# Decode attention with queries and probabilities as narrow stationary operands in four TensorE column groups

## The chip, the core and the metric

The program runs on one core of one Trainium2 chip. The metric is device time in microseconds (us) of one launch. The kernel before was timed three times: 375.3, 375.79 and 376.94 us, median 375.79 us. The profile is of a further execution, which took 379.11 us.

## What is computed

Two transformer layers are applied twice to four single tokens, with the same weights and the same caches in both passes. Cut to what matters:

```
x = A_x                                   # B=4 tokens, D=512
for pass in (1, 2):
    xn = layernorm(x)
    q  = (xn @ wq)  -> 32 heads of 128    # four query heads share one key/value head
    s  = q . k_cache * 128**-0.5          # per token 8 kv heads x 4096 keys x 128
    p  = softmax(s)
    x  = x + (p @ v_cache) @ wo
    xn = layernorm(x)
    x  = x + (gelu(xn @ w_gate) * (xn @ w_up)) @ w_down     # F=1792
return x
```

Everything is bf16 in memory. The key cache and the value cache are 33.5 MB each (4 tokens x 8 heads x 4096 x 128). The weights are 13.6 MB together.

## The kernel before

**Tiles.** A key or value tile is half of one kv head: 2048 rows, 512 KB, laid as 128 partitions x 16 rows x 128. `load_kv` (L101) issues each as one DMA on SP's queue into the pool `kvin`, which has `KV_BUFS = 7` buffers shared by keys and values. One queue carries everything, so the order of the calls in the program is the order of the transfers.

**Keys** (`keys`, L209). A head's 32 blocks of 128x128 are transposed on TensorE (L218: the key block is stationary, the identity streams), eight at a time into a PSUM tile `tp` (three buffers). `evac` copies each to SBUF as `kt`, two in five on ScalarE (L205), the rest on VectorE (L207). The pool `ktp` holds eight heads. They stay there, because pass 2 of the same token uses them again: keys are read from memory once.

**Scores** (`scores`, L222). The transposed key block is the stationary operand and the four query columns of its group stream past it: 32 matmuls of 4 columns for each head, result with the keys on the partitions. Two heads make a group (`GH = 2`, four groups `NGRP`), which has one `softmax` (L231): maximum along the free axis, `partition_all_reduce` on GpSimd, subtraction, exponential on ScalarE, sum, a second `partition_all_reduce`, reciprocal.

**Values** (`values`, L254). A block of 128 value rows is stationary, four probability columns stream past it: 32 matmuls of 4 columns for each head, accumulated in `ot` (one PSUM buffer), then one VectorE multiplication by the reciprocal writes the head's output, already transposed, into `OT_bf` (L264). Values are read twice, once in each pass.

**Order of the work.** The loop over tokens (L280) does pass 1 group by group: keys of two heads, scores, softmax, and the values of the group before. Then come the output projection (L159), the FFN (L164), a layer norm and the projection of pass 2's queries (`q_proj`, L303, 128 matmuls). Pass 2 of a token is deferred: its scores and softmaxes are done at once (L307), but its values are read after the next token's `q_proj` (L304 to L306), or for the last token at the end (L308). The `kt` buffers of a token come free only when its pass-2 scores are done. The framework's scheduler fixes the order on each engine when the program is built: it may take up work that comes later in the program where, by its own estimate, that work is ready, so matmuls of different steps are interleaved on TensorE. On the chip each engine then runs its instructions in that fixed order.

Of the kernel before, what the change touches and what calls it, by code (L numbers as in the profile page):

```python
# [8 lines left out]
FP32 = mybir.dt.float32  # L9
BF16 = mybir.dt.bfloat16  # L10
I32 = mybir.dt.int32
ACT = mybir.ActivationFunctionType
ALU = mybir.AluOpType
AX = mybir.AxisListType
RED = bass_isa.ReduceOp
# [6 lines left out]
GH = 2  # L22
KV_BUFS = 7
# [3 lines left out]
def kernel(  # L27
# [28 lines left out]
    NGRP = Hkv // GH  # L56
    assert Hkv % GH == 0 and C % CH == 0 and CH % TB == 0
    assert GH * C * rep * 4 <= 2048 and KF * B * 4 <= 2048 and Hq * B * 4 <= 2048
# [7 lines left out]
    p1p = ctx.enter_context(tc.tile_pool(name="p1p", bufs=3))  # L66
    p2p = ctx.enter_context(tc.tile_pool(name="p2p", bufs=NGRP + 1))
    shp = ctx.enter_context(tc.tile_pool(name="shp", bufs=2))
    grp = ctx.enter_context(tc.tile_pool(name="grp", bufs=2 * NGRP))
# [4 lines left out]
    ps_misc = ctx.enter_context(tc.tile_pool(name="ps_misc", bufs=2, space=bass.MemoryType.PSUM))  # L74

    ident_bf = const.tile([P, P], BF16, name="ident_bf")
    make_identity(nc, ident_bf[:])
    mean_f = const.tile([P, P], FP32, name="mean_f")
# [16 lines left out]
    q2_bf = state.tile([P, B, Hq], BF16, name="q2_bf")  # L95
# [44 lines left out]
    def q_proj(b0, nb, q_bf, parts):  # L140
        bs = slice(b0, b0 + nb)
        hp = Hq // parts
        for part in range(parts):
            qps = ps_misc.tile([P, hp, nb], FP32, name="qps", tag="misc")
            for i in range(hp):
                m = part * hp + i
                for k in range(KD):
                    nc.tensor.matmul(qps[:, i, :], lhsT=wq_sb[:, k, m * Dh:(m + 1) * Dh],  # L148
                                     rhs=xn_bf[:, bs, k], start=(k == 0), stop=(k == KD - 1))
            nc.vector.tensor_copy(  # L150
                out=q_bf[:, bs, part * hp:(part + 1) * hp].rearrange("p b h -> p h b"),
                in_=qps[:])
# [45 lines left out]

    KT = {}
# [9 lines left out]
    def keys(b, kvh):  # L209

        kt = ktp.tile([P, C, P], BF16, name="kt", tag="kt")
        KT[kvh] = kt
        for t in range(NT):
            kn = load_kv(A_k_cache, b, kvh, t, "k_t")
            for g in range(CH // TB):
                tp = ps_tp.tile([P, TB, P], BF16, name="tp", tag="tp")
                for i in range(TB):
                    nc.tensor.transpose(tp[:, i, :], kn[:, g * TB + i, :], ident_bf[:, :])  # L218
                c0 = t * CH + g * TB
                evac(kt[:, c0:c0 + TB, :], tp[:])  # L220

    def scores(b, g, q_bf):  # L222
        sc = ps_sc.tile([P, GH, C, rep], FP32, name="sc", tag="sc")
        for s in range(GH):
            kvh = g * GH + s
            for c in range(C):
                nc.tensor.matmul(sc[:, s, c, :], lhsT=KT[kvh][:, c, :],  # L227
                                 rhs=q_bf[:, b, kvh * rep:(kvh + 1) * rep], start=True, stop=True)
        return sc

    def softmax(sc, pool):  # L231
        colmax = grp.tile([P, GH, rep], FP32, name="colmax", tag="colmax", bufs=2)
        nc.vector.tensor_reduce(out=colmax[:], in_=sc.rearrange("p s c h -> p s h c"),  # L233
                                axis=AX.X, op=ALU.max)
        gmax = grp.tile([P, GH, rep], FP32, name="gmax", tag="gmax", bufs=2)
        nc.gpsimd.partition_all_reduce(gmax.rearrange("p s h -> p (s h)"),  # L236
                                       colmax.rearrange("p s h -> p (s h)"), P, RED.max)
        sh = shp.tile([P, GH, C, rep], FP32, name="sh", tag="sh")
        nc.vector.tensor_tensor(out=sh[:], in0=sc[:],  # L239
                                in1=gmax[:].unsqueeze(2).broadcast_to([P, GH, C, rep]),  # L240
                                op=ALU.subtract)
        pe = pool.tile([P, GH, C, rep], BF16, name="pe", tag="pe")
        nc.scalar.activation(out=pe[:], in_=sh[:], func=ACT.Exp, scale=scale)  # L243
        ssum = grp.tile([P, GH, rep], FP32, name="ssum", tag="ssum", bufs=2)
        nc.vector.tensor_reduce(out=ssum[:], in_=pe.rearrange("p s c h -> p s h c"),  # L245
                                axis=AX.X, op=ALU.add)
        den = grp.tile([P, GH, rep], FP32, name="den", tag="den", bufs=2)
        nc.gpsimd.partition_all_reduce(den.rearrange("p s h -> p (s h)"),  # L248
                                       ssum.rearrange("p s h -> p (s h)"), P, RED.add)
        rden = grp.tile([P, GH, rep], FP32, name="rden", tag="rden")  # L250
        nc.vector.reciprocal(out=rden[:], in_=den[:])
        return pe, rden

    def values(b, kvh, prob, o_bf):  # L254
        pe, rden = prob
        s = kvh % GH
        ot = ps_ot.tile([P, rep], FP32, name="ot", tag="ot")
        for t in range(NT):
            v = load_kv(A_v_cache, b, kvh, t, "v_t")
            for i in range(CH):  # L260
                c = t * CH + i
                nc.tensor.matmul(ot[:], lhsT=v[:, i, :], rhs=pe[:, s, c, :],  # L262
                                 start=(c == 0), stop=(c == C - 1))
        nc.vector.tensor_tensor(out=o_bf[:, b, kvh * rep:(kvh + 1) * rep], in0=ot[:],  # L264
                                in1=rden[:, s], op=ALU.mult)
# [4 lines left out]
    hq0 = GH * rep * Dh  # L270
# [8 lines left out]
    prob2_prev = None  # L279
    for b in range(B):  # L280
        prob1 = {}
        for g in range(NGRP):
            for s in range(GH):
                keys(b, g * GH + s)
            if b == 0 and g == 0:
                dq.dma_start(out=wq_sb[:, :, hq0:], in_=wq_dram[:, :, hq0:])
                q_proj(0, B, q1_bf, NGRP)
            prob1[g] = softmax(scores(b, g, q1_bf), p1p)
            if b == 0 and g == NGRP - 1:
                dq.dma_start(out=wo_sb[:], in_=A_wo.rearrange("(i p) n -> p i n", p=P))  # L290
            if g > 0:
                for s in range(GH):
                    values(b, (g - 1) * GH + s, prob1[g - 1], OT_bf)
        for s in range(GH):
            values(b, (NGRP - 1) * GH + s, prob1[NGRP - 1], OT_bf)
# [7 lines left out]
        q_proj(b, 1, q2_bf, 2)  # L303
        if prob2_prev is not None:  # L304
            for kvh in range(Hkv):
                values(b - 1, kvh, prob2_prev[kvh // GH], OT2_bf)  # L306
        prob2_prev = [softmax(scores(b, g, q2_bf), p2p) for g in range(NGRP)]  # L307
    for kvh in range(Hkv):  # L308
        values(B - 1, kvh, prob2_prev[kvh // GH], OT2_bf)
# [41 lines left out]
```

## Time and profile before

| | |
|---|---|
| median of three runs | 375.79 us |
| the profiled execution, whole | 379.11 us |
| its span, first to last instruction | 377.3 us |
| TensorE (PE) busy | 275.4 us, 73% |
| VectorE (DVE), ScalarE (ACT), GpSimd (POOL) busy | 137.5, 67.7, 25.0 us |
| mean granted TensorE clock | 0.648 |
| moved by DMA | 115.59 MB, 306 GB/s over the span |
| key transposes (L218), matmuls and busy time | 1024, 97.2 us |
| score matmuls (L227) | 2048, 69.3 us |
| value matmuls (L262) | 2048, 69.0 us |

PE is TensorE's matmul side and PEld its weight loads, which overlap. SPq is the queue on SP that issues the DMAs; a wait of SPq is a transfer that could not be issued yet. PEclk is the share of full speed that TensorE was granted. A group's busy time is the time in which at least one of its instructions ran, and the mean beside it is the length of one, from issue to end, so for pipelined matmuls the count times the mean is much more than the busy time.

### The profile page before, as it was taken

How to read it: one execution, taken by the hardware profiler on the slowest of the kernel's cores; microseconds unless marked ns; L12 is line 12 of the kernel's file. 1: busy time of each engine (PE TensorE's matmuls, PEld its weight loads, DVE VectorE, ACT ScalarE, POOL GpSimd, SP SyncE). 2: the span in 40 equal slices, each digit the busy share in tenths (PEclk: the TensorE clock that was granted, in tenths of full speed). 3: DMA queues.
4: the chain of work that ended last, by engine and by line, in shares of the span. 5: the costliest groups of instructions: out<-in, count | busy, mean ns of one | idle time of the engine just before them, and what ended most of it. 6: DMA issues, size and time to landing. Idle time of an engine off the chain costs nothing.

```text
span 377.3 us, 15723 instructions
## 1 busy us (share of the span) xinstructions
PE 275.4 (73%) x7268; PEld 263.8 (70%) x7268; DVE 137.5 (36%) x476; ACT 67.7 (18%) x90; POOL 25.0 (7%) x70
## 2 busy tenths in 40 slices
PE   0978872645999897578888885697978866785645
PEld 0878862535998896577788785697978865775545
DVE  0534440032456442333463433334534332351032
ACT  1314230000143330001242230001423400010000
POOL 0000000000112000001100000011010000020000
PEclk9999685555558667555596685555778855555555
DMA  7998999999258999947899999758999998579920
GB/s 283 413 370 271 387 353 382 406 377 394 83 164 269 384 347 347 386 122 220 279 407 406 356 361 410 244 179 241 404 365 349 377 373 302 156 218 347 407 109 4
DMA packets 35762, 115.59 MB, mean 306 GB/s; under 512 B 3176, under 2 KB 9072, under 8 KB 35696
## 3 DMA queue, kind: packets, MB, share of 16 engines
q1 hardware_dynamic: 35696, 114.58, 83.0%
q8 instruction: 57, 0.93, 1.0%
q14 instruction: 9, 0.07, 0.0%
HBM read 114.56 MB, written 0.00 MB: 304 GB/s over the span
## 4 chain that ended last, share of the span: by engine, by line
PE 53%; DMA 16%; DVE 15%; issue 9%; ACT 3%; POOL 3%; SPq 1%; POOLq 0%; ACTq 0%; DVEq 0%
PE tp L218 19%; PE sc L227 14%; DMA v_t<-in_A_v_cache_dram 9%; PE ot L262 7%; DMA wd_sb<-in_B_w_down_dram 6%; PE qps L148 4%; DVE kt L207 2%; PE yT L159 2%; PE hg L170 2%; DVE colmax L233 2%; DMA k_t<-in_A_k_cache_dram 2%; DVE ssum L245 2%; ACT kt L205 2%; ACT pe L243 1%; PE st L114 1%
## 5 line engine op out<-in xcount | busy, mean ns | idle before, releaser
L218 PE MATMUL tp<-ident_bf,k_t 128*128 128x128 bf16 x1024 | 97.2, 271 | 1.2 <-DMA k_t<-in_A_k_cache_dram 0.6
L218 PEld LDWEIGHTS <-k_t 128*128 128x128 bf16 x1024 | 85.2, 125 | 2.0 <-issue 1.0
L262 PE MATMUL ot<-pe,v_t 128*128 128x4 bf16 x2048 | 69.0, 166 | 17.0 <-DMA v_t<-in_A_v_cache_dram 9.7
L262 PEld LDWEIGHTS <-v_t 128*128 128x128 bf16 x2048 | 63.0, 102 | 19.1 <-DMA v_t<-in_A_v_cache_dram 11.0
L227 PE MATMUL sc<-q_bf,kt 128*128 128x4 bf16 x2048 | 69.3, 166 | 9.1 <-DVE kt L207 3.1
L227 PEld LDWEIGHTS <-kt 128*128 128x128 bf16 x2048 | 64.4, 102 | 12.8 <-DVE kt L207 5.3
L205 ACT COPY kt<-tp 128x1024 bf16<-128x1024 bf16 x52 | 52.6, 1012 | 111.0 <-PE tp L218 93.9
L207 DVE COPY kt<-tp 128x1024 bf16<-128x1024 bf16 x76 | 51.7, 687 | 53.2 <-PE tp L218 51.6
L159 PEld LDWEIGHTS <-wo_sb 128*128 128x128 bf16 x640 | 22.4, 102 | 27.8 <-issue 18.6
L159 PE MATMUL yT<-OT_bf,wo_sb 128*128 128x1 bf16 (+1 forms) x640 | 22.2, 165 | 25.5 <-DVE OT_bf L264 16.4
L243 ACT ACTIVATE pe<-sh 128x256 bf16<-128x256 f32 x32 | 13.3, 417 | 99.0 <-DVE sh L239 72.9
L236 POOL PARTITION_ALL_REDUCE gmax<-colmax x32 | 11.8, 369 | 266.6 <-DVE colmax L233 262.0
L264 DVE TENSOR_TENSOR OT_bf<-ot,rden 128x4 bf16<-128x4 f32 x64 | 9.6, 149 | 53.4 <-PE ot L262 53.4
L148 PE MATMUL qps<-xn_bf,wq_sb 128*128 128x1 bf16 (+1 forms) x640 | 18.4, 165 | 8.2 <-DVE xn_bf L136 6.6
L148 PEld LDWEIGHTS <-wq_sb 128*128 128x128 bf16 x640 | 17.9, 104 | 8.8 <-DVE xn_bf L136 7.1
L233 DVE TENSOR_REDUCE colmax<-sc 128x8 f32<-128x256 f32 x32 | 13.6, 424 | 28.0 <-PE sc L227 25.9
L239 DVE TENSOR_TENSOR sh<-sc,gmax 128x256 f32<-128x256 f32 x32 | 13.5, 423 | 11.0 <-POOL gmax L236 10.8
L170 PE MATMUL hg<-xn_bf,wg_sb 128*128 128x1 bf16 (+1 forms) x280 | 8.2, 165 | 10.8 <-DVE xn_bf L136 5.8
L245 DVE TENSOR_REDUCE ssum<-pe 128x8 f32<-128x256 bf16 x32 | 13.3, 415 | 7.5 <-ACT pe L243 7.5
L248 POOL PARTITION_ALL_REDUCE den<-ssum x32 | 13.2, 413 | 39.7 <-DVE ssum L245 39.4
L170 PEld LDWEIGHTS <-wg_sb 128*128 128x128 bf16 x280 | 7.9, 104 | 11.2 <-DVE xn_bf L136 5.0
L194 PEld LDWEIGHTS <-wd_sb 128*128 128x128 bf16 x280 | 8.1, 104 | 8.8 <-issue 5.2
(95 smaller groups left out, 83.1 us busy)
## 6 DMA issues: line engine op xcount, KB each, us to landing
v_t<-in_A_v_cache_dram SPq DMA_DIRECT2D x128, 512.0 KB, 7.1
k_t<-in_A_k_cache_dram SPq DMA_DIRECT2D x64, 512.0 KB, 6.5
wo_sb<-in_A_wo_dram SPq DMA_DIRECT2D x1, 4096.0 KB, 18.8
wq_sb<-in_A_wq_dram SPq DMA_DIRECT2D x1, 3072.0 KB, 15.5
wg_sb<-in_B_w_gate_dram SPq DMA_DIRECT2D x1, 1792.0 KB, 12.3
wu_sb<-in_B_w_up_dram SPq DMA_DIRECT2D x1, 1792.0 KB, 16.3
wd_sb<-in_B_w_down_dram SPq DMA_DIRECT2D x1, 1792.0 KB, 20.9
wq_sb<-in_A_wq_dram SPq DMA_DIRECT2D x1, 1024.0 KB, 5.1
```

Source lines behind the costliest of these rows:

```text
L148: nc.tensor.matmul(qps[:, i, :], lhsT=wq_sb[:, k, m * Dh:(m + 1) * Dh], rhs=xn_bf[:, bs, k], start=(k == 0), stop=(k == KD - 1))
L159: nc.tensor.matmul(yT[:, :, dk], lhsT=wo_sb[:, i, dk * P:(dk + 1) * P], rhs=o_bf[:, bs, i], start=(i == 0 and dk == 0), stop=(i == Hq - 1 ...
L170: nc.tensor.matmul(hg[:, m, :], lhsT=wg_sb[:, k, m * P:(m + 1) * P], rhs=xn_bf[:, bs, k], start=(k == 0), stop=(k == KD - 1))
L205: nc.scalar.copy(out=out_ap, in_=in_ap)
L207: nc.vector.tensor_copy(out=out_ap, in_=in_ap)
L218: nc.tensor.transpose(tp[:, i, :], kn[:, g * TB + i, :], ident_bf[:, :])
L227: nc.tensor.matmul(sc[:, s, c, :], lhsT=KT[kvh][:, c, :], rhs=q_bf[:, b, kvh * rep:(kvh + 1) * rep], start=True, stop=True)
L233: nc.vector.tensor_reduce(out=colmax[:], in_=sc.rearrange("p s c h -> p s h c"), axis=AX.X, op=ALU.max)
L239: nc.vector.tensor_tensor(out=sh[:], in0=sc[:], in1=gmax[:].unsqueeze(2).broadcast_to([P, GH, C, rep]), op=ALU.subtract)
L243: nc.scalar.activation(out=pe[:], in_=sh[:], func=ACT.Exp, scale=scale)
L245: nc.vector.tensor_reduce(out=ssum[:], in_=pe.rearrange("p s c h -> p s h c"), axis=AX.X, op=ALU.add)
L262: nc.tensor.matmul(ot[:], lhsT=v[:, i, :], rhs=pe[:, s, c, :], start=(c == 0), stop=(c == C - 1))
```

## The change

**Scores.** A PSUM tile `sc` of 128 x 512 now holds the scores of four heads (`GH = 4`, two groups instead of four). Row 32j + 8s + 4b + h is head s of the group, query h, and key block 2j + b of 512 keys. The stationary operand is a 128x32 slice of a zero-padded query tile `zq` (28 zeros, four query columns, 28 zeros), placed so that the four queries fall on the wanted rows and the other 28 rows get zeros added. Eight matmuls for each head stream 512 key columns each; four successive ones write the four row blocks 32j, that is four column groups of the array. **Softmax** works on packed rows: one maximum for each row, masks (`onehot`, `maskneg`) to combine rows of one query through `partition_all_reduce`, one exponential that also sums, then four TensorE transposes and a copy give `pT`, keys on the partitions. **Values.** The stationary operand is a 128x32 slice of `pT`; 256 value columns (two row blocks of 128) stream past it, 16 matmuls for each head, again four column groups in turn. The result holds wanted and unwanted rows; ScalarE copies it to SBUF as f32, two f32 transposes on TensorE turn it, and VectorE sums the eight wanted blocks and multiplies by the reciprocal.

**Order.** Values of the deferred pass 2: one head after the next token's keys 1 and one after keys 2, the other six after its `q_proj`. **Buffers.** `kvin` goes from 7 to 6. The PSUM pool `ps_misc` (layer norm, projections, FFN) goes from two buffers to one, and a new one-buffer pool `ps_t` takes both kinds of new transposes. The first part of `wq`, loaded ahead of the first keys, is half of it (2 MB) instead of a quarter.

```diff
-GH = 2
-KV_BUFS = 7
+GH = 4
+ZP = 28
+KV_BUFS = 6
...
+    pTp = ctx.enter_context(tc.tile_pool(name="pTp", bufs=4))
+    osp = ctx.enter_context(tc.tile_pool(name="osp", bufs=1))
...
-    ps_misc = ctx.enter_context(tc.tile_pool(name="ps_misc", bufs=2, space=bass.MemoryType.PSUM))
+    ps_t = ctx.enter_context(tc.tile_pool(name="ps_t", bufs=1, space=bass.MemoryType.PSUM))
+    ps_misc = ctx.enter_context(tc.tile_pool(name="ps_misc", bufs=1, space=bass.MemoryType.PSUM))
...
+    def scores(sc, kvh, zq):
+
+        s = kvh % GH
+        for kbp in range(2):
+            off = ZP - rep * (2 * s + kbp)
+            for j in range(4):
+                nc.tensor.matmul(sc[32 * j:32 * j + 32, :], lhsT=zq[:, kvh, off:off + 32],
+                                 rhs=KT[kvh][:, 2 * j + kbp].rearrange("p c k -> p (c k)"),
+                                 start=(s == 0 and kbp == 0), stop=(s == GH - 1 and kbp == 1),
+                                 skip_group_check=True)
+
+    def softmax(sc):
+        m = grp.tile([P, 1], FP32, name="m", tag="m")
+        nc.vector.tensor_reduce(out=m[:], in_=sc[:], axis=AX.X, op=ALU.max)
...
+        nc.gpsimd.partition_all_reduce(gm[:], am[:], P, RED.max)
...
+        nc.scalar.activation(out=pr.rearrange("p c k -> p (c k)"), in_=sc[:], func=ACT.Exp,
+                             bias=nb[:, 0:1], scale=scale, accum_out=ls[:])
+        ptp = ps_t.tile([P, NCC, P], BF16, name="ptp", tag="t")
+        for cc in range(NCC):
+            nc.tensor.transpose(ptp[:, cc, :], pr[:, cc, :], ident_bf[:, :])
+        pT = pTp.tile([P, NCC, P], BF16, name="pT", tag="pT")
+        nc.vector.tensor_copy(out=pT[:], in_=ptp[:])
...
+        ot = ps_ot.tile([P, 2, Dh], FP32, name="ot", tag="ot")
         for t in range(NT):
...
+            for cl in range(CT):
+                cc = t * CT + cl
+                for j in range(4):
+                    nc.tensor.matmul(ot[32 * j:32 * j + 32, :, :],
+                                     lhsT=pT[:, cc, 32 * j:32 * j + 32], rhs=v[:, j, cl],
+                                     start=(cc == 0), stop=(cc == NCC - 1))
+        os = osp.tile([P, 2, Dh], FP32, name="os", tag="os")
+        nc.scalar.copy(out=os[:], in_=ot[:])
+        oT = ps_t.tile([P, 2 * P + 8], FP32, name="oT", tag="t")
+        for k in range(2):
+            nc.tensor.transpose(oT[:, k * P:(k + 1) * P], os[:, k, :], ident_f[:, :])
...
+        nc.vector.tensor_reduce(out=od[:], in_=sel, axis=AX.XY, op=ALU.add)
+        nc.vector.tensor_tensor(out=o_bf[:, b, kvh * rep:(kvh + 1) * rep], in0=od[:],
                                 in1=rden[:, s], op=ALU.mult)
...
+        for kvh in range(GH):
+            keys(b, kvh)
...
+            scores(sc, kvh, z1)
+            if kvh in (1, 2):
+                old_values(1)
+        p0 = softmax(sc)
+        sc = new_scores()
+        for kvh in range(GH, Hkv):
+            keys(b, kvh)
+            scores(sc, kvh, z1)
+            values(b, kvh - GH, p0, OT_bf)
+        p1 = softmax(sc)
...
+        for kvh in range(GH, Hkv):
+            values(b, kvh, p1, OT_bf)
...
+        old_values(Hkv)
+        prob2 = []
+        for g in range(2):
+            sc = new_scores()
+            for s in range(GH):
+                scores(sc, g * GH + s, zq2)
+            prob2.append(softmax(sc))
```

## The prediction, made before the changed kernel was run

> **What bounds the kernel now.** I read the page's engine lines first, then its slices, a table of busy time by stage, SPq's waits, and single stretches of TensorE's timeline.
>
> ```profile
> PE 275.4 (73%) x7268; PEld 263.8 (70%) x7268; DVE 137.5 (36%) x476; ACT 67.7 (18%) x90; POOL 25.0 (7%) x70
> ...
> PEclk9999685555558667555596685555778855555555
> DMA  7998999999258999947899999758999998579920
> ```
>
> TensorE is the busiest engine, but the DMA line stands at 9 except in four dips and at the end. The stage table cuts the span at the ends of output projections and at the next token's first key transposes (columns: PE, PEld, DVE, ACT, POOL busy; PEclk; DMA share; GB/s):
>
> ```profile
> 10.00:88.30 78.30, 51.34 (x1144) 48.98 (x1143) 27.05 (x87) 15.04 (x18) 3.09 (x8) 0.74 1.01 371
> ...
> 100.90:149.60 48.70, 43.77 (x1023) 42.51 (x1019) 23.00 (x57) 15.08 (x20) 5.71 (x15) 0.68 0.81 281
> 149.60:183.80 34.20, 23.74 (x812) 23.09 (x812) 12.60 (x62) 1.88 (x5) 3.01 (x8) 0.50 0.71 246
> 183.80:229.50 45.70, 38.97 (x903) 36.94 (x900) 19.59 (x47) 14.82 (x17) 3.05 (x8) 0.76 1.00 380
> ```
>
> Token 0 (first line) is all DMA: its weights come down the same queue. Pass 1 of tokens 1 and 2 (second and last line; token 3 took 44.9 us) is near both limits, with PE busy 85 to 90%. The stage after each (third line; 34.8 and 34.1 us for tokens 2 and 3) leaves the DMA at 0.71. SPq says why:
>
> ```profile
> SPq L104 <- PE ot L262: 100.6, 74, 5.7
> SPq L104 <- PE tp L218: 97.8, 59, 11.1
> ```
>
> A tile is fetched when TensorE is done with an older one. In the timeline, seven of the 16 value tiles of the deferred token are used before the queries are ready at 168.5, and nine after, among the scores; the next keys are transposed only at 183.8. The order of TensorE's queue bounds this stage.
>
> **Prices.** First two pieces of the chain, then two of the timeline, then the only f32 matmuls:
>
> ```profile
> 102.28 1.69 PE sc L227 x64
> 183.97 1.73 PE tp L218 x16
> ...
> 188.02 1.07 PE L218 MATMUL tp<-ident_bf,k_t 128*128 128x128 bf16 x16
> 188.93 0.34 PE L227 MATMUL sc<-q_bf,kt 128*128 128x4 bf16 x8
> ...
> L114 PE MATMUL st<-xx,mean_f x20: 350/362/422, 10.7 to 364.9; 128*128 128x8 f32 x16, 128*128 128x32 f32 x4
> ```
>
> A 4-column matmul takes 26 ns of queue time. A 128-column one takes 108 ns where the clock is 0.50 (0.84 ns a column), and 57 ns in the warm stretch, (188.93 - 188.02) / 16, 0.44 ns a column. In token 2's pass 1, L218 was busy 22.15 us for 256, 0.68 ns a column. The clock is 0.50 in stages of narrow matmuls only and 0.76 where 128-column ones are frequent; the change makes almost all attention work wide, so I take 0.56 ns, midway between 0.68 and 0.44.
>
> **What is removed** per head: 32 score and 32 value matmuls, 0.84 us each set. **What is added:**
>
> *Scores*: 8 matmuls x 512 columns. The trace has no two matmuls in different column groups. If four run together: 2 x 512 x 0.56 = 0.57 us; one after another: 2.29 us. The nearest row, narrow matmuls of 166 ns spaced 26 ns, shows that one need not end before the next starts, so I take together. *Values*: 16 x 256 columns, again 0.57 or 2.29 us.
>
> The Trainium skill, "TensorE: Matmul & The Clock Gate", Part 3, measured 2.38 times for three column tiles, 79% of perfect. By that figure (an estimate) the scores and the values of a head would cost 0.15 us more each, 128 x 0.15 = 19 us in all before what the DMA covers. Against the change, "TensorEngine Tiling (Array Packing)", Key Properties, says that switching between tiling modes drains the array, without a price; the kernel switches twice for every block of scores or values.
>
> *Fill at each such block*: an isolated matmul takes 166 ns instead of 26, so up to 0.14 us at each end, 0 to 0.28 us; I take 0.15, the middle. *f32 transposes*, two for each head's values: the layer norm's f32 matmul comes as two instructions (20 for 10 calls). From 8 to 32 columns it grows from 362 to about 410 ns, 2 ns a column, so 128 columns stream in 0.26 us; one transpose costs 0.26 us if it is one instruction, 0.52 if two. Two of them: 0.5 to 1.05, I take 0.9, nearer to the only f32 row. *Softmax*: four 128-column transposes, 0.3 us, 16 softmaxes instead of 32.
>
> So a head's values cost 0.57 + 0.15 + 0.9 = 1.6 us instead of 0.84, a head's scores 0.72 instead of 0.84.
>
> *Waits that are new on TensorE.* Between a head's values and its transposes stands ScalarE's copy of 128x256 (0.42 as L243, plus 0.2 us of handover on each side), 0.8 us; `ot` has one buffer, so the next head's values are held as well. While keys are in the queue they fill it; at the last four heads of a pass half is filled: 1.5 us. Between scores and values stand two VectorE steps, GpSimd's reduction, the exponential and the transposes: the like chain from 54.54 to 56.47 takes 1.9 us up to the end of the exponential, with 256 columns; with 512 and one more step about 3. The first softmax is covered by keys, the second not: 3 us.
>
> *Pass 1*, tokens 1 to 3, now with ten heads' values: keys 256 x 128 x 0.56 = 18.4, scores 8 x 0.72 = 5.8, values 10 x 1.6 = 16.2, softmax transposes 0.6, output projection 4.5 (as before), waits 4.5: 50.0 us. The DMA needs 36 tiles x 1.28 us (512 KB at the 410 GB/s of the fullest slices) = 46.1, so PE ends last. Against 48.7, 45.7 and 44.9: +1.3, +4.3, +5.1 = **+10.7**. Token 0: eight heads x 0.8 more lie in the 27 us in which PE idles there; **+2** for the first half, which has keys alone to transpose.
>
> *The stage after*: the FFN chain is the same. The deferred values shrink from 16 tiles to 12, so the first key tile is asked for four tiles earlier. After the queries: scores 8 x (2 x 512 x 0.84 ns + 0.15) = 8.1 us at clock 0.50, plus three heads at 2 us = 14 instead of 15.3, and the keys may start among them: -4 a token. `ps_misc` with one buffer makes the up projection wait for the gate's copy (0.17 plus handover) and the second half of the queries for the first's: +1. Three stages: **-9**.
>
> *End*: eight heads' values at 2.2 to 3 us against 2.56 us of DMA for two tiles: **+2**. Behind the last tile: copy, transposes, reduction and the single `ps_misc`: **+2.5**.
>
> *At nothing*: one buffer less (a lone tile lands in 3.5 us, so three in flight keep the queue full; if it bites, up to 1.3 us a stage); masks and zeros at the start, and 1 MB more of `wq` first, beside the first 9.9 us in which PE waits for the identity; VectorE and ScalarE (ScalarE gains 64 x 0.42 = 27 us on 67.7).
>
> Sum: 379.1 + 2 + 10.7 - 9 + 2 + 2.5 = 387.3 for the profiled execution, which stands 0.9% above the median; on the median's scale **384 us**.
>
> **Rivals.**
>
> *A, the forecast*: groups run together, pass 1 becomes TensorE's. 384, own range 372 to 400. 44%.
>
> *B, faster*: the wide streams keep the clock near full (0.44 ns) and the short scores let the next keys in early. Pass 1: 14.4 + 4.8 + 14 + 0.5 + 4.5 + 4 = 42, under the DMA's 46.1, so about 47: -1.7, +1.3, +2. The stage after: scores in 8 x 0.6 = 4.8 us, keys at 5 instead of 15 us behind the queries: -10 each. With +2 at the end 379.1 - 26 = 353, about 350 on the median's scale. For it: the clock line's 9 and 8 stand in key stages. Against: 0.50 whenever the FFN has just idled PE. It decides from about 0.50 ns a column, where pass 1 falls under the DMA. 30%.
>
> *C, slower by more*: no warm stretch (0.84), fills of 0.28, transposes of 1.05. Pass 1: 27.5 + 8 x 1.14 + 10 x 2.2 + 0.9 + 4.5 + 4.5 = 68, +66 in all; +9, +6 elsewhere: 460 at worst, with half of it 415. 16%.
>
> *D, the change doesn't do what it says*: the groups take turns. Each head's scores and values cost 1.72 us more, 32 times for each token, 220 us less what the DMA covers: 550 to 600. For it: no row shows otherwise. 10%.
>
> **Numbers.** A measurement of this kernel can tell about 0.5% from no change, 2 us. Faster: B and 0.09 of A, 0.39. Within: 0.09 of A. Slower: the rest, 0.52. The range leaves out D and the ends of B and C: 345 to 430.
>
> **What would show it.** Together or in turn: four score matmuls start within 0.1 us of each other, or 0.3 to 0.4 apart. f32 transposes: 128 instructions or 256, and PE busy of 0.5 or 1 us a head. Pass-1 stages: 50 us with the DMA share under 0.95 (A), 47 near 1.0 (B), 60 or more (C). Clock in pass 1: about 0.85 (A), near 1 (B). Stage after: 31 us (A) or 24 (B). I am wrong if pass 1 doesn't lengthen, or if the stage after grows because PE waits for ScalarE's copy with nothing to fill it.

## The result and the profile after

The changed kernel takes 393.73 us (median of four runs, 392.77 to 396.5) beside 376.37 us (375.3 to 380.78) for the kernel before in the same comparison. The ratio is 1.045, with a 95% interval of 1.035 to 1.0551: slower by 4.5%, where 2.2% was forecast. Times here are medians of all executions, while ratios and intervals use only those in the faster of two states that executions of one kernel fall into, so the two can differ by a few tenths of a percent. The profiled execution of it took 393.11 us, with a span of 391.4 us.

The engine lines and slices of the changed kernel's page:

```profile
PE 289.8 (74%) x4900; PEld 195.3 (50%) x4900; DVE 136.9 (35%) x538; ACT 90.6 (23%) x154; POOL 13.9 (4%) x38
...
PEclk9999995555699995558898985559999955575555
DMA  7978999999179999766699899567899997678800
```

TensorE issues a third fewer matmuls and is busy 14 us longer. Its clock is at 9 or 8 in the key stages. The DMA line has more 7s and 6s: bytes come more slowly although there are no more of them. The stage table (columns as before) for pass 1 of token 1, pass 1 of token 2, the stage after token 2, and pass 1 of token 3:

```profile
93.92:157.92 64.00, 52.06 (x845) 34.98 (x845) 25.81 (x83) 19.78 (x31) 3.31 (x8) 0.82 0.83 310
...
186.37:241.89 55.52, 43.37 (x651) 31.12 (x648) 20.95 (x58) 19.11 (x29) 2.09 (x5) 0.84 0.92 336
241.89:270.88 28.99, 24.89 (x476) 15.69 (x470) 10.30 (x60) 3.22 (x9) 1.21 (x3) 0.60 0.70 235
270.88:324.31 53.43, 41.22 (x651) 28.23 (x648) 21.11 (x58) 18.93 (x29) 2.09 (x5) 0.90 0.94 352
```

In pass 1 of token 2 PE is busy 43.4 of 55.5 us, and the DMA is no longer at 1.00: neither ends the stage alone. SPq waits longer for value matmuls, 142.8 us instead of 100.6:

```profile
SPq L126 <- PE ot L310: 142.8, 94, 4.3
```

Cut the same way in both profiled executions (each stage from the end of an output projection, or the first key transposes behind it, to the next such mark), the spans compare like this; the last column is the forecast's change. The row of token 1 also holds token 0's second queries and scores, in both kernels, because token 1's first keys are transposed ahead of them; the forecast's +1.3 was worked out from a cut that begins at 100.90:

| stage | before, us | after, us | change | forecast |
|---|---|---|---|---|
| token 0: pass 1, then its FFN | 65.7 + 15.3 | 70.8 + 13.1 | +2.9 | +2 |
| pass 1 of token 1 | 58.8 | 64.0 | +5.2 | +1.3 |
| pass 1 of token 2 | 45.4 | 55.5 | +10.1 | +4.3 |
| pass 1 of token 3 | 47.4 | 53.4 | +6.0 | +5.1 |
| stages after tokens 1 and 2 | 34.0 + 32.2 | 28.5 + 29.0 | -8.7 | -6 |
| last: the stage after token 3 and its deferred values | 55.5 | 53.7 | -1.8 | -1 |
| tail | 13.0 | 13.4 | +0.4 | +2.5 |
| span | 377.3 | 391.4 | +14.1 | +8.2 |

All of the miss lies in pass 1 of tokens 1 to 3: +21.3 instead of +10.7. The other stages did better than forecast by 4.7 us. (What of the +21.3 is only moved work is answered by e8 below.) The rest of the gap between 4.5% and 2.2% is that the two profiled executions stand differently to their medians: the one before 0.7% above, the one after 0.2% below.

What the 55.5 us of token 2's pass 1 hold, by TensorE's groups in that window (busy, mean ns, then the idle time before them and what ended it):

```profile
L250 PE MATMUL tp<-ident_bf,k_t 128*128 128x128 bf16 x256 | 19.8, 238 | 0.4 <-ACT kt L237 0.4
L310 PE MATMUL ot<-v_t,pT 128*32 128x256 bf16 x168 | 11.6, 318 | 1.4 <-DVE pT L288 1.4
L264 PE MATMUL sc<-kt,zq_0_129 128*32 128x512 bf16 x64 | 7.5, 383 | 3.5 <-ACT kt L237 2.0 <-DVE kt L239 1.1
L317 PE MATMUL oT<-ident_f,os 128*128 128x128 f32 x20 | 5.4, 360 | 5.2 <-ACT os L314 5.2
L188 PE MATMUL yT<-OT_bf,wo_sb 128*128 128x1 bf16 x128 | 4.6, 165 | 0.2 <-DVE OT_bf L323 0.2
L286 PE MATMUL ptp<-ident_bf,pr 128*128 128x128 bf16 x15 | 1.8, 245 | 1.5 <-ACT pr L282 1.5
```

The last column adds up to 12.2 us of waits: 5.2 for the copy of a head's output (ten heads, 0.52 each, with keys in the queue or not), 3.5 for copies of transposed keys, 3 for the softmax. That is the term that the forecast had at 4.5. The busy times of the six groups add up to 50.7 us, for 43.4 us in which TensorE was busy at all, because groups overlap at their ends.

Where values run alone, TensorE's timeline shows one head:

```profile
150.32 0.69 PE L317 MATMUL oT<-ident_f,os 128*128 128x128 f32 x2 [0.53 <-ACT os L314]
...
150.94 0.62 PE L310 MATMUL ot<-v_t,pT 128*32 128x256 bf16 x8
...
151.49 0.58 PE L188 MATMUL yT<-OT_bf,wo_sb 128*128 128x1 bf16 x16
...
152.73 0.37 ACT L314 COPY os<-ot 128x256 f32<-128x256 f32 x1 [2.46 <-PE ot L310]
...
153.16 0.69 PE L317 MATMUL oT<-ident_f,os 128*128 128x128 f32 x2 [0.53 <-ACT os L314]
```

From transposes to transposes are 2.84 us, for two tiles that take the DMA 2.56. In the kernel before the same work keeps the DMA's pace, and PE waits for the tile:

```profile
352.53 0.58 PE L262 MATMUL ot<-pe,v_t 128*128 128x4 bf16 x16 [0.69 <-DMA v_t<-in_A_v_cache_dram]
...
355.09 0.58 PE L262 MATMUL ot<-pe,v_t 128*128 128x4 bf16 x16 [0.70 <-DMA v_t<-in_A_v_cache_dram]
```

### The profile page after: what moved, and what is told of

Read it like the earlier page. It is cut to its first block, busy times and chain, and to the rows that moved or that the text cites. A ratio compares the mean times of both kernels' runs of the same rounds, so it can differ in the third digit from the quotient of the medians.

```text
span 391.4 us, 11136 instructions
## 1 busy us (share of the span) xinstructions
PE 289.8 (74%) x4900; PEld 195.3 (50%) x4900; DVE 136.9 (35%) x538; ACT 90.6 (23%) x154; POOL 13.9 (4%) x38
## 4 chain that ended last, share of the span: by engine, by line
PE 52%; DVE 15%; ACT 11%; DMA 11%; issue 6%; POOL 2%; SPq 1%; ACTq 0%; POOLq 0%
PE ot L310 11%; PE tp L250 10%; PE sc L264 9%; PE oT L317 6%; ACT kt L237 5%; DMA wd_sb<-in_B_w_down_dram 5%; PE qps L174 5%; PE yT L188 4%; DMA k_t<-in_A_k_cache_dram 4%; ACT os L314 3%; ACT pr L282 3%; DVE m L271 3%; DVE kt L239 3%; DMA v_t<-in_A_v_cache_dram 2%; PE hg L199 2%
## 5 line engine op out<-in xcount | busy, mean ns | idle before, releaser
L310 PE MATMUL ot<-v_t,pT 128*32 128x256 bf16 x1024 | 76.9, 349 | 6.3 <-DVE pT L288 5.2
L250 PE MATMUL tp<-ident_bf,k_t 128*128 128x128 bf16 x1024 | 76.4, 232 | 2.5 <-ACT kt L237 1.2
L250 PEld LDWEIGHTS <-k_t 128*128 128x128 bf16 x1024 | 66.3, 105 | 12.0 <-issue 9.5
L314 ACT COPY os<-ot 128x256 f32<-128x256 f32 x64 | 23.8, 372 | 161.0 <-PE ot L310 161.0
L317 PE MATMUL oT<-ident_f,os 128*128 128x128 f32 x128 | 37.0, 383 | 28.3 <-ACT os L314 28.0
L322 DVE TENSOR_REDUCE od<-oT 128x4 f32<-128x32 f32 x64 | 12.2, 190 | 111.2 <-PE oT L317 110.9
L317 PEld LDWEIGHTS oT<-ident_f,os 128*128 128x128 f32 x128 | 16.1, 176 | 53.4 <-ACT os L314 53.4
L310 PEld LDWEIGHTS <-pT 128*32 128x32 bf16 x1024 | 28.0, 104 | 26.2 <-issue 14.0
L264 PE MATMUL sc<-kt,zq_131 128*32 128x512 bf16 x256 | 27.0, 506 | 0.0
L264 PE MATMUL sc<-kt,zq_1_130 128*32 128x512 bf16 x128 | 15.3, 384 | 6.0 <-DVE kt L239 3.3
L264 PE MATMUL sc<-kt,zq_0_129 128*32 128x512 bf16 x128 | 15.2, 398 | 5.5 <-ACT kt L237 2.7
L271 DVE TENSOR_REDUCE m<-sc 128x1 f32<-128x512 f32 x16 | 10.8, 678 | 16.8 <-PE sc L264 16.8
L282 ACT ACTIVATE pr<-sc,nb 128x512 bf16<-128x512 f32 x16 | 11.0, 687 | 19.8 <-DVE am L278 12.6
```

Of the source, the lines that this page charges most:

```text
L250: nc.tensor.transpose(tp[:, i // CT, i % CT, :], kn[:, g * TB + i, :], ident_bf[:, :])
L264: nc.tensor.matmul(sc[32 * j:32 * j + 32, :], lhsT=zq[:, kvh, off:off + 32], rhs=KT[kvh][:, 2 * j + kbp].rearrange("p c k -> p (c k)"), st ...
L271: nc.vector.tensor_reduce(out=m[:], in_=sc[:], axis=AX.X, op=ALU.max)
L282: nc.scalar.activation(out=pr.rearrange("p c k -> p (c k)"), in_=sc[:], func=ACT.Exp, bias=nb[:, 0:1], scale=scale, accum_out=ls[:])
L310: nc.tensor.matmul(ot[32 * j:32 * j + 32, :, :], lhsT=pT[:, cc, 32 * j:32 * j + 32], rhs=v[:, j, cl], start=(cc == 0), stop=(cc == NCC - 1))
L314: nc.scalar.copy(out=os[:], in_=ot[:])
```

## The experiments

Each ratio is to the kernel before in the same comparison, with its 95% interval. "Turning" is what follows a head's value matmuls: the copy `os`, the transposes `oT` and the sum of eight blocks.

### Do the column groups run together?

**e4_in_turn.** The loops over column group and key block are exchanged in scores and values, so that two successive matmuls share a group (0, 0, 1, 1, 2, 2, 3, 3).

```diff
-        for kbp in range(2):
-            for j in range(4):
+        for j in range(4):
+            for kbp in range(2):
```

> The same matmuls as the changed kernel, but with the loops over column group and key block exchanged, so that successive matmuls fall into the same column group, both for scores (two in a row) and values (two in a row). If different groups run together in the changed kernel (spacing 0.09 to 0.1 us for 512 columns): a block of eight score matmuls goes from 0.75 or 1.5 us to about 1.3 or 2.6, values likewise, and the time rises by 30 to 90 us. If they take turns already: no change within 2 us.

One execution: 398.76 us, 5 us above the changed kernel. The expectation for groups that run together failed, and so did the reading behind it. A count of score matmuls running in short stretches of the changed kernel (in parentheses; a matmul counts in each stretch that it touches):

```profile
100.50:100.52 0.02, 0.01 (x4) 0.01 (x4) 0.50 0.00 0
100.52:100.90 0.38, 0.38 (x4) 0.12 (x8) 0.50 0.00 0
100.90:100.95 0.05, 0.05 (x8) 0.04 (x4) 0.50 0.00 0
```

Four start within 20 ns, and the next four 0.4 us later. That they do run together shows in the time of many in a row:

```profile
100.51 5.77 PE L264 MATMUL sc<-kt,zq_131 128*32 128x512 bf16 x61
```

These take about 0.1 us each; one after another, at the 0.84 ns a column that the forecast read at clock 0.50, each would take 0.43. In the same place with the loops exchanged:

```profile
101.98:102.34 0.36, 0.36 (x4) 0.13 (x8) 0.50 0.00 0
102.34:102.40 0.06, 0.06 (x8) 0.04 (x4) 0.50 0.00 0
```

Still four at a time. If matmuls started strictly in the program's order, at most two could have run together (the second of one group and the first of the next). It is different where a head's keys become ready in two halves, as in pass 1 (first e4, then the changed kernel):

```profile
26.69 0.61 PE L264 MATMUL sc<-kt,zq 128*32 128x512 bf16 x4
27.56 0.61 PE L264 MATMUL sc<-kt,zq 128*32 128x512 bf16 x4
...
26.79 0.39 PE L264 MATMUL sc<-kt,zq_0_129 128*32 128x512 bf16 x2
27.68 0.61 PE L264 MATMUL sc<-kt,zq_0_129 128*32 128x512 bf16 x6
```

The views don't name a matmul's column group, but the split of the eight (4 and 4, 2 and 6) fits the loops' order in each kernel. In e4 a half brings four matmuls of only two groups, which take 0.61 us, as long as six in the changed kernel. Over the launch the scores keep TensorE busy for 62.5 instead of 57.5 us, about what the kernel lost. So the order costs something where half a block is ready and nothing that can be seen where all of it is, and rival D is out.

### What does the turning cost?

**e1_no_turn.** The turning is left out.

```diff
-        os = osp.tile(...); nc.scalar.copy(out=os[:], in_=ot[:])
-        oT = ...; 2 x nc.tensor.transpose(...); nc.vector.tensor_reduce(out=od[:], ...)
-        nc.vector.tensor_tensor(out=o_bf[...], in0=od[:], ...)
+        nc.vector.tensor_tensor(out=o_bf[...], in0=ot[:, 0, 0:rep], ...)
```

> The packed values without the turning of their output: no ScalarE copy, no f32 transposes, no selection; VectorE multiplies four columns of the unturned result by the reciprocal instead, so the attention output is not the reference's. Theory T (the turning is the loss: TensorE stands 0.53 us for each copy and spends 0.3 us on each f32 transpose, so values go at 2.84 us a head, slower than their DMA): values alone go at the DMA's 2.56 us a head, the pass-1 stages fall from 55.5 and 53.4 us to 46 to 48, time 365 to 375. Rival S (streaming the values wide at half clock costs the time): pass 1 stays above 52, time above 385. Rival B (six tile buffers and groups of four heads starve the DMA): time above 385.

379.05 us, ratio 1.0012 (0.9965 to 1.0058): as fast as the kernel before. That lies between theory T (365 to 375) and its rivals (above 385), and pass 1 of tokens 2 and 3 falls to 50.5 and 49.1 us, not to 46 to 48. The turning is worth 4.4% of the time, some 15 us, and it is not all that is lost. PE's own busy time for it is about 37 us over the launch and its waits are 28, so most of these 65 us had been covered.

**e2_narrow_values.** Scores and softmax as changed, values as before (value block stationary, four columns of `pT` stream), so there is nothing to turn.

```diff
+            for i in range(CH):
+                nc.tensor.matmul(ot[:], lhsT=v[:, i, :], rhs=pT[:, t * CT + cl, r:r + rep], ...)
```

> The changed kernel with packed scores and softmax, but values as before: the value block stationary, four probability columns of the turned probabilities streaming, output already turned. Theory T: as without the turning, 362 to 375, near the run without turning, since 32 narrow matmuls take 0.84 us and 16 packed ones 0.7 to 1.05. Rival S: faster than the run without turning by 8 us or more. Rival B: above 385.

388.71 us, 1.0314 (1.0236 to 1.0392): not theory T's 362 to 375, but in the range of rival B (above 385), which blames the buffers and the groups of four. This has no turning either, yet it is 3% slower than e1. With its output computed in full it stands 1.3% under the changed kernel by the ratios, whose intervals just overlap. Its stage table for pass 1 of tokens 2 and 3:

```profile
186.97:243.34 56.37, 45.96 (x778) 36.42 (x776) 18.66 (x46) 14.62 (x17) 2.07 (x5) 0.71 0.90 314
...
273.48:322.21 48.73, 39.31 (x779) 30.55 (x776) 18.58 (x47) 14.41 (x17) 2.10 (x5) 0.90 0.97 357
```

The same matmuls took 56.4 us at clock 0.71 and 48.7 at 0.90. Streaming the values wide, before the turning is paid for, is a gain of about 3%, by e1 against e2; that it comes by way of the clock is what these two rows suggest, not more.

**e3_turn_bf16.** `os` and `oT` in bf16 instead of f32.

```diff
-        os = osp.tile([P, 2, Dh], FP32, ...)
+        os = osp.tile([P, 2, Dh], BF16, ...)
```

> The changed kernel with the output copied and transposed in bf16 instead of f32. Theory T, its wait part larger than its transposes: the 0.53 us wait stays, the pair of transposes falls from 0.44 to 0.69 us to 0.2 to 0.35, so 2.84 becomes about 2.5 us a head where only values run, under the DMA's 2.56: 382 to 388. If the f32 transposes are the whole loss: 375 to 380. Rivals S and B: no change, 391 to 394.

404.59 us, 1.071 (1.0636 to 1.0784): slower by 11 us with cheaper transposes, outside every range that was expected. The timeline says why:

```profile
155.25 0.38 PE L188 MATMUL yT<-OT_bf,wo_sb 128*128 128x1 bf16 x9 [0.48 <-DVE OT_bf L323]
...
157.53 0.40 PE L317 MATMUL oT<-ident_bf,os 128*128 128x128 bf16 x2 [0.53 <-ACT os L314]
...
158.41 0.38 PE L188 MATMUL yT<-OT_bf,wo_sb 128*128 128x1 bf16 x9 [0.48 <-DVE OT_bf L323]
```

The pair takes 0.40 instead of 0.69 us. But the fixed order now has a head's output projection right behind its transposes, where it waits 0.48 us for VectorE; with f32 the next head's first eight value matmuls stood between them. Over the launch 33 such waits take 17.4 us, and the period of a head becomes 158.41 - 155.25 = 3.16 us.

**e5_one_score_buf** and **e6_two_out_bufs.** `ot` gets a second PSUM buffer, taken from the scores; e5 is the control with the scores' buffer taken and not used.

```diff
-    ps_sc = ctx.enter_context(tc.tile_pool(name="ps_sc", bufs=2, ...))
-    ps_ot = ctx.enter_context(tc.tile_pool(name="ps_ot", bufs=1, ...))
+    ps_sc = ctx.enter_context(tc.tile_pool(name="ps_sc", bufs=1, ...))
+    ps_ot = ctx.enter_context(tc.tile_pool(name="ps_ot", bufs=2, ...))
```

> The changed kernel with one PSUM buffer for scores instead of two, nothing else: the control for the next run, which needs the bank. Theory T: scores of the next group wait for the exponential of the one before, some 2 us in each of 16 places, half of it covered: 394 to 408. If the order of the work shifts little: 392 to 396.

> As the control with one score buffer, and the freed bank given to a second buffer for the values' result, so that the next head's values need not wait for ScalarE's copy. Theory T in the form that the wait of 0.53 us a head is the loss (28 us of TensorE's idle time in all): 8 to 20 us under the control. If the f32 transposes and the longer pass through ScalarE and VectorE are the loss and the wait only shows where TensorE had nothing else: within 3 us of the control.

391.52 us, 1.04 (1.0336 to 1.0464), and 393.04 us, 1.0426 (1.0346 to 1.0507). The control came out just under both of its expected ranges: a second score buffer is worth nothing here. The buffer alone does nothing: TensorE's order still has the transposes right behind their own head's values, and its waits for the copy stay (26.8 us, as in the control's 26.9).

**e9_turn_later.** On top of e6, a head's transposes are issued behind the next head's value matmuls.

```diff
+        turn_last()            # the head before: transposes, sum, multiplication
         os = osp.tile(...)
         nc.scalar.copy(out=os[:], in_=ot[:])
+        pending.append(turn)
```

> As the run with one score buffer and two output buffers, but the two f32 transposes of a head are issued behind the next head's value matmuls instead of behind its own. Theory Q (the wait for ScalarE's copy comes from TensorE's fixed order, in which the transposes follow their own head at once, not from the buffer): the idle time of the transposes behind the copy falls from 27 to under 8 us, a head in the values-only stretches from 2.84 to 2.3 to 2.6, time 378 to 386. Rival (the f32 transposes and the later stages hold it anyway): within 3 us of 391 to 393.

391.2 us, 1.042 (1.033 to 1.0509): no gain over e6 that can be told. But the wait was not taken away either: the transposes' wait for the copy fell from 26.8 to 21.5 us only, where under 8 was expected, and TensorE's wait for the softmax's exponential rose from 12.1 to 21.8. So this run does not show what the wait itself is worth. **e10_select** replaces the transposes and the sum by two bf16 matmuls of four columns against a 0/1 selection matrix; **e11_select_later** does both, with e6's buffers.

```diff
-            nc.tensor.transpose(oT[:, k * P:(k + 1) * P], os[:, k, :], ident_f[:, :])
-        nc.vector.tensor_reduce(out=od[:], in_=sel, ...)
+            nc.tensor.matmul(oT[:], lhsT=os[:, k, :], rhs=selb[:, k, s * rep:(s + 1) * rep], ...)
```

> The changed kernel with the two f32 transposes and VectorE's sum of eight blocks replaced by two bf16 matmuls of four columns against a constant selection matrix, which turn and sum at once; the copy is in bf16, one output buffer, two score buffers. Theory T by size (the transposes are 0.6 us of 2.84 a head): 380 to 387. Rival from the bf16 turning (the scheduler puts the output projection's matmuls right behind and they wait 0.48 us for VectorE): 390 to 402.

> Selection by matmul and issued behind the next head's values, with two output buffers and one score buffer: both parts of the turning taken off TensorE's path. Theories T and Q: near the run without any turning, 373 to 382, values-only stretches at the DMA's 2.56 us a head. Rival (something else in the packed form costs 15 us): above 386.

390.4 us, 1.036 (1.0257 to 1.0463), and 388.67 us, 1.0345 (1.0256 to 1.0435). By their medians these recover 3 to 5 of the 15 us, less than expected, and their intervals overlap with the changed kernel's. The range of e11's rival came (above 386), but not its reason: e1 has the rest of the packed form at the time of the kernel before. TensorE's waits in e11:

```profile
PE ptp L294 <- ACT pr L290: 24.0, 15, 2.4
PE oT L333 <- ACT os L329: 19.0, 36, 0.5
```

The wait for the copy has fallen from 28.0 us in the changed kernel (26.8 in e6) to 19.0, and the wait for the softmax's exponential has grown from 6.2 (12.1 in e6) to 24.0. That work which had covered the one no longer covers the other is a reading of these sums, not shown by a run.

### Does the order of the deferred values matter?

**e7_late_all_after** takes the two heads of deferred values out of the changed kernel's pass 1; **e8_before_moved** gives the kernel before the changed order (one head after keys 1, one after keys 2, six after the queries).

```diff
-            if kvh in (1, 2):
-                old_values(1)
```

> The changed kernel, but all eight heads of deferred values after the queries, none among the next token's keys. Theory O (moving two heads' values only shifts their 5 us of DMA from the stage after to pass 1): pass 1 falls from 55 to about 50 us, the stage after rises from 28.5 to 33, time 388 to 398. Rival G (in groups of four heads the first half of pass 1 has keys alone; without the moved values the DMA idles there): pass 1 stays at 53 or more, time above 400.

> The kernel before with nothing of the change but its order of the deferred values: one head after keys 1, one after keys 2, six after the queries. Theory O: the stage after falls by 4 to 6 us a token and pass 1, at a DMA share of 1.0, grows by as much: 372 to 380. Rival (the stage after is the only slack and pass 1 has room): 360 to 368. Rival (TensorE has no room in pass 1): above 384.

393.48 us, 1.0405 (1.0306 to 1.0505), and 378.37 us, 1.0025 (0.9979 to 1.007). The order is neutral in both. In e7 pass 1 of tokens 2 and 3 falls to 51.5 and 50.7 us. Pass 1 of token 2 in e8:

```profile
180.00:231.59 51.59, 44.05 (x960) 42.01 (x960) 20.09 (x49) 14.71 (x17) 3.45 (x9) 0.67 0.95 355
```

Pass 1 of token 3 takes 52.9 us there, and the stage after tokens 1 and 2 takes 27.3 and 28.9. So most of what the stage table shows as lost in pass 1 and won behind it is only these heads, moved. Against the one profiled execution of e8, which has the same order, the changed kernel's span is 17.3 us longer: 4.7 in token 0, 0.5, 3.9 and 0.5 in pass 1 of tokens 1 to 3, 1.3 in the stages after tokens 1 and 2, 5.9 in the last stage, where most values run alone, and 0.5 in the tail.

### What is a tile buffer worth?

**e12_five_bufs**: the changed kernel with five buffers. **e13_before_six**: the kernel before with six. **e14_space_six**: the changed kernel with 3.5 KB of SBUF saved elsewhere, a control. **e15_space_seven**: the same with seven. **e16_before_half**: the kernel before with half tiles and 14 buffers.

```diff
-KV_BUFS = 6
+KV_BUFS = 5                 # e12; in the kernel before 7 -> 6 (e13); e14 -> e15: 6 -> 7
...
-CH = 16                     # e16, from the kernel before
-KV_BUFS = 7
+CH = 8
+KV_BUFS = 14
```

> The changed kernel with five tile buffers instead of six. Rival B (the step from seven to six cost several us): the next step costs at least as much, above 398. Theory T: the buffers matter only where the DMA is the limit, 391 to 397.

> The kernel before with six tile buffers instead of seven, nothing else. Rival B (the places for tiles set how far the DMA runs ahead while TensorE is held, and the step costs as it does from six to five): 384 to 392. Theory T alone (at nothing, as in the prediction): 375 to 379.

> The control for the next run: the changed kernel with 3.5 KB of SBUF saved (three instead of four buffers of turned probabilities, one instead of two query tiles, the output copy in the buffer of the probabilities, small tiles shared), still six tile buffers. Expected 391 to 399: new order, but no new work.

> As the control, with the space given to a seventh tile buffer. Rival B: 8 to 14 us under the control, 380 to 388. Theory T alone: within 3 us of the control, as TensorE is the limit wherever values run.

> The kernel before with tiles of half the size (256 KB, 1024 rows) and fourteen buffers, the same space and bytes. If the limit is how early a buffer's space comes free (rival B by places): a tile is released after 16 or 8 matmuls instead of 32 or 16 and the dips fill earlier, 360 to 372. If the number of bytes ahead is all that counts: 374 to 379. If shorter rows (2 KB instead of 4 KB a partition) and twice the issues slow the queue: above 380.

| | us | ratio (interval) |
|---|---|---|
| e12, changed, five | 406.4 | 1.0788 (1.068 to 1.0897) |
| changed, six | 393.73 | 1.045 (1.035 to 1.0551) |
| e14, changed, six, space saved | 393.35 | 1.0458 (1.038 to 1.0536) |
| e15, changed, seven | 388.44 | 1.0344 (1.0272 to 1.0416) |
| e13, before, six | 386.15 | 1.0277 (1.0181 to 1.0373) |
| e16, before, 14 half tiles | 381.54 | 1.0142 (1.0092 to 1.0192) |

A buffer that the forecast had at nothing is worth 13 us from five to six and 5 from six to seven in the changed kernel, and 10 us (2.8%) from six to seven in the kernel before. The saved space itself changes nothing (e14). The 5 us of e15 lie between its two expectations (8 to 14, and under 3). TensorE's waits for tiles in the kernel before, first with six buffers, then with seven:

```profile
PE ot L262 <- DMA v_t<-in_A_v_cache_dram: 15.5, 20, 2.3
PE tp L218 <- DMA k_t<-in_A_k_cache_dram: 4.7, 3, 1.7
...
PE ot L262 <- DMA v_t<-in_A_v_cache_dram: 9.7, 13, 2.2
PE tp L218 <- DMA k_t<-in_A_k_cache_dram: 0.6, 1, 0.6
```

With one buffer less TensorE waits 9.9 us more for tiles that have not landed, about the size of the loss (the two spans differ by 6.6 us). Half tiles in the same bytes (e16) gain nothing and lose 1.4%. That speaks against places being the limit, but this run also halves the rows and doubles the DMA issues, and it fell in the range that was expected if these slow the queue, so it does not show that bytes alone count.

### Do the two losses add up?

**e17_no_turn_seven** is e1 with seven buffers (the turning left out again); **e18_select_later_seven** is e11 with seven, its output computed in full.

> The changed kernel without the turning of the output (as in the run without turning, it leaves out the copy, the transposes and the sum of eight blocks, and multiplies four columns of the unturned result instead) and with seven tile buffers instead of six. Theory S, the two losses add up: turning 15 us and the missing buffer 5 us, so 379 - 5 = 374 us, 372 to 376, below the kernel before. Rival T, they are one loss seen twice, since both act by tiles that come free late: without the turning nothing is held back and the seventh buffer is worth under 2 us: 377 to 379.

> The output turned by two 4-column matmuls against a selection matrix, issued behind the next head's value matmuls, two output buffers in PSUM, and seven tile buffers; the output is computed in full. Theory S, savings add up: 388.7 for the same with six buffers less 5 for the seventh = 384 us, 381 to 386. Rival T, the moved waits bound the kernel whatever is prefetched: 387 to 389. Both stay slower than the kernel before.

369.16 us, 0.9842 (0.9796 to 0.9888), and 385.09 us, 1.0269 (1.0227 to 1.031). Theory S holds for e17, which went past its range: without the turning the seventh buffer is worth 1.7%, not less. There T, one loss seen twice, falls. e18 came in S's range too, but by the ratios its buffer is worth 0.7% (e11 against e18), and these two intervals overlap. SPq's waits for value matmuls are down to 116.1 us. Pass 1 of tokens 2 and 3 in e17:

```profile
179.13:225.50 46.37, 35.60 (x619) 26.40 (x616) 18.30 (x47) 14.55 (x17) 2.10 (x5) 0.93 0.97 368
...
253.93:301.80 47.87, 38.27 (x618) 27.41 (x616) 18.71 (x46) 14.44 (x17) 2.08 (x5) 0.89 0.95 360
```

These two stages take 46.4 and 47.9 us at clock 0.93 and 0.89 with the DMA near 1: what rival B had described. Case A's own sum says the same of a pass 1 without turning: 50.0 less 9 and 1.5 us lies under the DMA's 46.1. What the change does apart from the turning and the buffer saves time; it is spent on these two. What saves seems to be the wide values: e2, with wide scores and narrow values at six buffers, stands at 1.0314, no better than the kernel before at six (e13, 1.0277).

## Why the prediction was right and where it was wrong

**Direction and form: right.** Case A said that pass 1 becomes TensorE's and grows, that the stage after shrinks, and that the sum is a loss. Its signs came: clock 0.84 and 0.90 in pass 1, DMA share 0.92 and 0.94, the stage after at 28.5 and 29.0 us (31 was forecast). But of the 21.3 us by which pass 1 grows, e8, where only the order is changed, has 16.3 too (the forecast had counted these heads in), and what the changed kernel loses against e8 does not lie in pass 1 alone.

**Together or in turn: right.** Four score matmuls start within 20 ns. The sentence that cited the Trainium skill's 2.38 times for three column tiles ("TensorE: Matmul & The Clock Gate", Part 3) would have added 19 us. Here a second set of four follows the first after 0.4 us, as one 512-column matmul alone would at this clock by the forecast's 0.84 ns a column (0.43 us), so nothing of those 19 us shows. Nor is a gap to be seen between whole-array transposes and a block of wide matmuls, where the forecast had put a fill: in the timeline of one head above, value matmuls start at 150.94, before the transposes of 150.32 are recorded as ended.

**TensorE's work in pass 1: the sum right, its terms less so.** 45.5 us forecast, 43.4 and 41.2 measured. Turning is cheaper than forecast: one instruction for each transpose (128 in all), 5.4 us busy for ten heads where 9 had been put. The others are dearer as groups (keys 19.8 against 18.4, scores 7.5 against 5.8), but groups overlap by 7.3 us, so that the closeness of the sum is in part luck.

**The failed step: "waits 4.5".** Measured are 12.2 us in token 2's pass 1 and 12.2 (53.4 - 41.2) in token 3's. The forecast let keys fill the queue during the copy of a head's output, save for half of four heads. In the changed kernel all ten heads of token 2's pass 1 pay 0.52 us. The order is fixed when the program is built; work that could fill a wait does so only if it stands there, and the lines of e3 show the same thing from the other side. It also put nothing down for scores that wait for key copies (3.5 us, 1.0 in the kernel before). This is an account of TensorE's time and does not prove that the waits set the stage's length: e17's pass 1 of token 2 has 10.8 us of idle TensorE (46.4 - 35.6) with the DMA near 1. What is shown is the price of the whole turning, copy, transposes, sum and waits: 4.4% (e1).

**The second failed step: "At nothing: one buffer less".** The argument was that a lone tile lands in 3.5 us, so that three in flight keep the queue full, and its bound was 1.3 us a stage. It left out that a buffer is held not only in flight but also until TensorE is done with its tile. Measured: 1.1% in the changed kernel, 1.7% in it without the turning, 2.8% in the kernel before, where TensorE's waits for tiles grow by 9.9 us. That finished tiles in store carry the two engines over stretches in which one does other things is the likely reason; no run varied such a stretch.

**Smaller terms.** Values at the end at 2.2 to 3 us a head: 2.84. Token 0: +2.9 for +2. Tail: +0.4 for +2.5. Order of the deferred values: the forecast's -4 a token was moved work, not saved work; pass 1 got it back, as the forecast's ten heads had allowed for.

**The sum of it.** From the kernel before, by ratios: all of the change without turning at seven buffers -1.6% (e17), a buffer less +1.7% (e1 against e17), turning +4.4% (the changed kernel against e1): +4.5%. The other way round, turning +5.1% at seven buffers (e15 against e17) and a buffer less +1.1% (e15 against e14). The two are additive within these intervals.

**What stays open.** Why turning that is issued later or made of two narrow matmuls wins back so little (e9 to e11, and 16 us still lie between e17 and e18) is only argued: waits for the softmax grow in its place and the wait for the copy stays at 19 us or more, but no run took that wait away or held the softmax fixed while the turning moved. Nor is it shown which part of the turning, the copy or the longer hold on `ot`, SPq's longer waits come from.

## What to carry to other kernels

Before a stationary operand is made narrower, count what its unwanted output rows cost to turn back on the same engine: here the rest of the change gained 1.6%, and one copy, two transposes and one sum for each head took 4.4 to 5.1%. Don't price a prefetch buffer by the landing time of a transfer: here that gave nothing, and 1.1 to 2.8% was measured. Take one away in the kernel before and measure, since that single run (e13) would have told. Where the order on an engine is fixed at build time, a wait is covered only by what stands next in that order; ask for each new wait what is queued directly behind it, not what work exists.

## What was not expected of the hardware

The order in which matmuls of the four column groups stand in the program mattered little. With two successive ones in the same group (e4) four still ran at a time where all eight of a block were ready, while starting strictly in order would have allowed two; the kernel lost 5 us (one execution), about what its half blocks explain. The Trainium skill ("TensorE: Matmul & The Clock Gate", Part 3) says that matmuls start and end strictly in program order; the stretches shown for e4 disagree, if the built program keeps the loops' order, as its half blocks suggest, and the measurement decides.

The granted clock did not follow the busy share. In the changed kernel's pass 1 of token 1 PE is busy 52.06 of 64.00 us (81%) at clock 0.82. The kernel before, in the same stage, has it busy 90% at 0.65:

```profile
90.98:149.82 58.84, 52.81 (x1281) 51.20 (x1281) 26.83 (x74) 16.09 (x21) 6.08 (x16) 0.65 0.77 269
```

What differs is the kind of work: streams of 256 and 512 columns instead of 4. That this is the cause is not shown: in e2 the same matmuls ran at 0.71 in one token's pass 1 and at 0.90 in the next one's.
